# Fused attention and mixer kernel on one core: the transposes of the 64-key tile for two query tiles at a time, GpSimd's move taken out, and a new order

## The chip, the cores and the metric

The kernel runs on one core of one Trainium2 chip. The metric is the device time of one execution in microseconds (us); less is better. A core has five engines that run their own instruction streams and wait for each other through semaphores: TensorE (PE; its weight loads are listed apart as PEld), VectorE (DVE), ScalarE (ACT), GpSimd (POOL) and SyncE (SP, which here issues all DMAs).

## The reference, cut to what matters

```python
def _attn_ref(q, k, v, f):                  # B, H, S, D = 8, 8, 576, 64
    scores = np.matmul(q, k.transpose(0, 1, 3, 2)) / np.sqrt(D)
    cum = np.cumsum(np.log(np.clip(f, 0.0001, 1.0)), axis=-1)
    decay = cum[:, :, :, None] - cum[:, :, None, :]
    scores = np.where(causal, -1e9, scores + decay)     # causal: key after query
    attn = np.exp(scores - np.max(scores, axis=-1, keepdims=True))
    attn = attn / (np.sum(attn, axis=-1, keepdims=True) + 1e-09)
    return np.matmul(attn, v)

def _moe_ref(x, w_tok1, w_tok2, w_ch1, w_ch2):          # x: (8, 576, 512)
    h = np.maximum(x.transpose(0, 2, 1) @ w_tok1, 0.0) @ w_tok2     # 576 -> 256 -> 576
    u = x + h.transpose(0, 2, 1)
    return u + np.maximum(u @ w_ch1, 0.0) @ w_ch2                   # 512 -> 1536 -> 512
```

The 64 (batch, head) pairs go through causal attention with a decay; the result, laid out as (8, 576, 512), goes through a token-mixing and a channel-mixing block. The inputs are float32.

## The kernel before, in words

**Heads and tiles.** A loop in `build` goes over the 64 heads. The 576 positions of a head are five tiles: tile 0 has 64 positions, tiles 1 to 4 have 128 each. For each query tile `score` (L1061) makes the scores of all keys up to its end, `rmin` (L1068, DVE) adds the mask and takes the minimum, `expo` (L1075, ACT) writes the exponentials to a buffer `pr` and their sums, DVE makes reciprocals (L1093, L1096), and `norm` (L1103, POOL) multiplies the query tile's row of `pr` by its reciprocal: five instructions for a head, of 576, 448, 320, 192 and 64 columns.

**Transposes.** The product with `v` needs the normalised probabilities with keys on the partitions, so TensorE transposes them block by block (`tr`, L1117), a block being one query tile by one key tile: ten blocks for key tiles 1 to 4 (`trs`), and five for key tile 0. Of those five, the block of query tile 0 rides with the run of key tile 2, and `trs0` makes the other four, each 64 keys by 128 queries into one PSUM bank. There are 15 transposes for a head, 960 in all.

**Two parts of each number.** The matmuls take operands rounded to a shorter format, so 60 of the heads (all but the first four, called `fv` in the code) split a value into a high and a low part: ACT copies the transposed block from PSUM (high, `hi_act`, L729) and DVE subtracts that from PSUM (low, `lo_dve`, L738). Key tile 0 has only 64 keys, so its high part fills partitions 0 to 63 of a buffer `p0` and its low part is wanted in partitions 64 to 127, where one matmul (`av0`, L1189 and L1190) takes both. DVE writes the low part to a buffer `low` of 64 partitions, and POOL moves `low` to the upper half of `p0` (`hi_pool`, L732). `av0` waits for this move, and `avj` (L1197, L1199, L1201) adds the products of the other key tiles. In the first four heads nothing is split, and one copy suffices.

**The rest.** After every four heads of a batch `mixer` puts the token mixing and a part of the channel mixing of that batch into the same streams (L1683 to L1820). When the heads are done, the larger part of the channel mixing follows (L1544 to L1608). Weights are decoded and split by ACT, DVE and POOL beside the heads. `idle` (L803) puts small matmuls without use where the planner sees TensorE unoccupied.

**What sets the order.** `Plan.op` collects operations with a priority from the table `PR`; `Plan.run` simulates the engines and decides, for each engine, in which order the operations are written out; each buffer kind (`pr` has 3 buffers, `p0` and `low` have 1) is handed out on the way. In the kernel before, each engine takes, of the operations that are ready, the one with the lowest priority number.

## Time and profile before

| what | value |
|---|---|
| time, median of 3 runs | 1028.75 us (1024.6, 1028.75, 1030.69) |
| span of the profiled execution | 1021.2 us, 19368 instructions |
| PE busy | 1007.6 us, 99% |
| PEld busy | 882.6 us, 86% |
| DVE busy | 813.4 us, 80% |
| ACT busy | 694.8 us, 68% |
| POOL busy | 421.4 us, 41% |
| chain that ended last | PE 82%, DVE 7%, ACT 4%, POOL 2%, DMA 2%, issue 2% |

The own time of the profiled execution is not listed beside its span; the runs lie 3.4 to 9.5 us above the span, the median 7.5 us. The shares are means over two stages: in the first some 550 us the heads run, and all engines work; POOL has nothing after 600 us.

### The profile page before, as it was taken

The page shows a single profiled execution, that of the slowest core. Times are in us where ns is not written, and L with a number is a line of the kernel's source. Part 1 is how long each engine was busy: PE and PEld are TensorE (multiplying, and loading weights), DVE is VectorE, ACT ScalarE, POOL GpSimd, SP SyncE. Part 2 cuts the span into 40 slices and gives each one's busy share as a digit, 9 for nine tenths or more (in the row PEclk, how much of TensorE's full clock was granted, in tenths as well). Part 3 has the DMA queues.
Part 4 walks back from the last instruction along what each step waited for, and adds up shares of the span by engine and source line. Part 5 has one row for each costly group of instructions (what it writes and reads, how often), then busy time and mean ns, then how long its engine had stood idle before and what let it go on. Part 6 is the DMA issues. An engine that isn't in the chain of part 4 may idle for free.

```text
span 1021.2 us, 19368 instructions
## 1 busy us (share of the span) xinstructions
PE 1007.6 (99%) x6228; PEld 882.6 (86%) x6228; DVE 813.4 (80%) x1932; ACT 694.8 (68%) x1708; POOL 421.4 (41%) x530
## 2 busy tenths in 40 slices
PE   8999999999999999999999999999999999999998
PEld 6588998999999999999999988888888888888886
DVE  7789889888999887987896557959669766976694
ACT  6898888888988787878896444664375546544552
POOL 6689778687787686877881100000000000000000
PEclk9999999999999999999999999999999999999999
DMA  8765788876787766554665467825832762474154
GB/s 235 253 214 200 280 307 269 292 266 253 252 280 288 254 224 235 196 192 149 218 222 200 163 225 252 288 73 195 259 103 84 231 210 83 139 250 138 31 171 139
DMA packets 110597, 212.23 MB, mean 208 GB/s; under 512 B 13296, under 2 KB 51184, under 8 KB 109472
## 3 DMA queue, kind: packets, MB, share of 16 engines
q1 hardware_dynamic: 110496, 210.99, 61.4%
q8 instruction: 50, 0.82, 0.3%
q14 instruction: 51, 0.42, 0.1%
HBM read 113.26 MB, written 44.04 MB: 154 GB/s over the span
## 4 chain that ended last, share of the span: by engine, by line
PE 82%; DVE 7%; ACT 4%; POOL 2%; DMA 2%; issue 2%; SPq 0%; DVEq 0%; POOLq 0%; ACTq 0%
PE bank L1117 8%; PE bank L1606 6%; PE bank L1607 6%; PE bank L1544 6%; PE bank L1608 6%; PE bank L1545 6%; PE bank L1546 6%; PE bank L1061 5%; PE pair L1199 2%; PE pair L1061 2%; PE pair L1201 2%; ACT pr L1075 2%; PE bank L1785 2%; PE bank L1787 2%; PE bank L1786 2%
## 5 line engine op out<-in xcount | busy, mean ns | idle before, releaser
L1103 POOL TENSOR_SCALAR pr<-pr,rec 128x192 f32<-128x192 f32 (+4 forms) x320 | 165.6, 532 | 65.4 <-DVE rec L1096 27.3
L729 ACT ACTIVATE p<-bank 128x384 fp32r<-128x384 f32 (+3 forms) x300 | 129.1, 474 | 21.6 <-PE bank L1117 18.7
L1117 PE MATMUL bank<-ident,pr 128*128 128x128 f32 (+1 forms) x960 | 139.4, 274 | 1.8 <-DVE ring L738 1.0
L1075 ACT ACTIVATE pr<-bank,nmin 128x320 f32<-128x320 f32 (+3 forms) x256 | 118.3, 470 | 14.3 <-DVE nmin L1068 13.4
L1117 PEld LDWEIGHTS bank<-ident,pr 128*128 128x128 f32 (+1 forms) x960 | 106.4, 131 | 18.4 <-ACT pr L1075 2.5
L1068 DVE CUSTOM_DVE_ANT_0 bank<-bank,mask 128x448 f32<-128x448 f32 (+3 forms) x256 | 106.3, 434 | 14.5 <-PE bank L1061 9.4
L738 DVE TENSOR_TENSOR p<-bank,p 128x384 fp32r<-128x384 f32 (+1 forms) x180 | 105.0, 590 | 10.5 <-ACT p L729 9.4
L1606 PE MATMUL bank<-ring,w2r 128*128 128x512 f32 x242 | 94.2, 389 | 0.4 <-issue 0.4
L1607 PE MATMUL bank<-ring,w2r 128*128 128x512 f32 x242 | 94.2, 389 | 0.0
L1608 PE MATMUL bank<-ring,w2r 128*128 128x512 f32 x234 | 91.2, 390 | 0.0
L1061 PE MATMUL bank<-k 128*128 128x320 f32 (+1 forms) x480 | 83.1, 302 | 0.4 <-ACT pr L1075 0.2
L1201 PE MATMUL pair<-p,vv 128*128 128x512 f32 x240 | 75.6, 322 | 0.0
L980 POOL TENSOR_TENSOR hl<-raw,hl 128x1152 fp32r<-128x1152 f32 x27 | 72.3, 2678 | 1.1
L729 ACT ACTIVATE ring<-h 128x512 fp32r<-128x512 f32 x73 | 44.5, 628 | 41.3 <-PE bank L1608 16.0
L1199 PE MATMUL pair<-p,vv 128*64 128x512 f32 x240 | 69.4, 330 | 0.0
L729 ACT ACTIVATE ring<-xt 128x512 fp32r<-128x512 f32 (+1 forms) x83 | 52.3, 648 | 23.8 <-DVE xt L1512 8.4
L1061 PEld LDWEIGHTS bank<-k 128*128 128x128 f32 (+1 forms) x480 | 62.9, 176 | 3.9 <-DVE low L738 1.0
L738 DVE TENSOR_TENSOR low<-bank,p 64x512 fp32r<-64x512 f32 (+1 forms) x120 | 52.7, 443 | 8.8 <-ACT p L729 7.0
L729 ACT ACTIVATE ring<-bank 128x288 fp32r<-128x288 f32 (+2 forms) x96 | 46.9, 498 | 17.6 <-PE bank L1787 6.9
L1075 ACT ACTIVATE pr<-pair,nmin 128x576 f32<-128x576 f32 x64 | 47.3, 739 | 15.0 <-DVE nmin L1068 12.7
L735 POOL TENSOR_TENSOR ring<-xt,ring 128x576 fp32r<-128x576 f32 x32 | 45.8, 1439 | 21.6 <-ACT ring L729 20.4
L1606 PEld LDWEIGHTS bank<-ring,w2r 128*128 128x128 f32 x242 | 45.4, 188 | 10.3 <-ACT w2r L729 0.8
(197 smaller groups left out, 3046.9 us busy)
## 6 DMA issues: line engine op xcount, KB each, us to landing
k<-hl SPq DMA_DIRECT2D x180, 288.0 KB
w2r<-sd SPq DMA_DIRECT2D x80, 256.0 KB
raw<-in_qk SPq DMA_DIRECT2D x60, 288.0 KB
w2r<-wd SPq DMA_DIRECT2D x60, 256.0 KB
vr<-in_v SPq DMA_DIRECT2D x32, 320.0 KB
ud<-xt SPq DMA_DIRECT2D x8, 1152.0 KB
pd<-part SPq DMA_DIRECT2D x32, 288.0 KB
dd<-in_w_ch SPq DMA_DIRECT2D x12, 512.0 KB
```

The source lines that it names most:

```text
L729: nc.scalar.activation(out, in_, func, scale=scale)
L738: nc.vector.tensor_tensor(out, in_, asf(hi), op=ALU.subtract)
L1061: nc.tensor.matmul(ps[:m, of : of + w], k[:, 0, i0 : i0 + m], k[:, 1, j0 : j0 + w], start=(x == 0), stop=(fq or x == 1))
L1068: nc.vector.tensor_tensor_reduce(x, x, E["mask"][:m, a : a + w], -1.0 / D**0.5, 3e38, op0=ALU.add, op1=ALU.min, accum_out=E["nmin"][sm][:m ...
L1075: nc.scalar.activation(at(pr)[:m, poff[t] : poff[t] + w], at(buf)[:m, of : of + w], AF.Exp, bias=E["nmin"][sm][:m, t : t + 1], scale=-1.0, ...
L1103: nc.gpsimd.tensor_scalar(x, x, r, 0.0, op0=ALU.mult, op1=ALU.add)
L1117: nc.tensor.transpose(out, at(pr)[:, poff[i] + start[j] : poff[i] + end[j]], E["ident"])
L1199: nc.tensor.matmul(x[:D], at(vv)[:, v0 + j, :D], at(pb)[:, 1, c0 : c0 + w], start=False, stop=last)
L1201: nc.tensor.matmul(x, at(vv)[:, v0 + j, :], at(pb)[:, 0, c0 : c0 + w], start=False, stop=last)
L1606: nc.tensor.matmul(o_, wh[:, ms], h_, start=first and pr == 0, stop=False, skip_group_check=not first)
L1607: nc.tensor.matmul(o_, wl[:, ms], h_, start=False, stop=False, skip_group_check=not first)
L1608: nc.tensor.matmul(o_, wh[:, ms], l_, start=False, stop=pr == PH - 1, skip_group_check=not first)
```

## The change

The five transposes of key tile 0 become three. The blocks of query tiles 1 and 3 are put side by side, and so are those of 2 and 4: `norm` writes the 64 columns of key tile 0 of query tile 1 not in place but into 64 new columns of `pr` just ahead of query tile 3's row (and those of tile 2 ahead of tile 4's row). One transpose of 128 columns then takes the block of query tile 1 to partitions 0 to 63 and that of query tile 3 to partitions 64 to 127. The block of query tile 0 is a transpose of 64 by 64 (before, 128 rows of which half were zero). Of the result the lower PSUM half holds 320 queries and the upper half 256. ACT and DVE write the parts from each half straight to where they belong: the high part to the half that it came from, the low part to the other one. `low` and POOL's move are gone. `av0` is unchanged but for what it waits for.

For this `norm` becomes seven instructions for a head: 576, 448, 256, 128, 64 columns, and two more of 64 columns.

Beside it `Plan.run` is rewritten: each engine now takes its operations strictly by priority number, so `PR`, whose numbers are new, is the order itself. The number of small matmuls at the start is worked out from the planned start and no longer 112.

```diff
-    k19=(11, 23, 47, 59, 67, 77, 89, 104, 114, 142, 156, 174, 195, 211, 229, 256, 271, 285, 302, 328, 343, 360, 373, 394, 410, 421, 438, 455, 465, 478, 491, 502,),
...
+    poff = [sum(end[:t]) + T0 * max(0, t - 2) for t in range(NS)]
+    MID = T0 + 2 * P
...
-        def norm(t, sm=sm, pr=pr):
+        def norm(t, a, z, to, sm=sm, pr=pr):
             m = size[t]
-            x = at(pr)[:m, poff[t] : poff[t] + end[t]]
...
+            x, y = (at(pr)[:m, c : c + z - a] for c in (poff[t] + a, to))
+            nc.gpsimd.tensor_scalar(y, x, E["rec"][sm][:m, t // 2, t % 2 : t % 2 + 1], 0.0, op0=ALU.mult, op1=ALU.add)
...
         for t in (4, 3, 2, 1, 0):
+            a = T0 if t in (1, 2) else 0
+            p.op("POOL", d_pts(end[t] - a, 1), n + o["nrm"], lambda t=t, a=a, f=norm: f(t, a, end[t], poff[t] + a), rd=[("rec", sm)], wr=[(pr, t)], bufs=[pr])
+            if a:
+                p.op("POOL", d_pts(a, 1), n + o["nrm"], lambda t=t, a=a, f=norm: f(t, 0, a, poff[t + 2] - a), rd=[("rec", sm), (pr, t, "e")], wr=[(pr, t, "z")], bufs=[pr])
...
-                if first:
-                    tr(at(ps)[:T0, w : w + P], 0, 0)
...
-        def trs0(ps=ps, tr=tr):
-            for i in range(1, NS):
-                tr(at(ps)[:T0, (i - 1) * P : i * P], i, 0)
+        def trs0(ps=ps, pr=pr):
+            x, y = at(ps), at(pr)
+            nc.tensor.transpose(x[:T0, :T0], y[:T0, :T0], E["ident"][:T0, :T0])
+            for z in (0, 1):
+                nc.tensor.transpose(x[:, T0 + z * P : T0 + (z + 1) * P], y[:, poff[z + 3] - T0 : poff[z + 3] + T0], E["ident"])
...
+            for z, hs, ls, cs, ds in ((0, slice(0, T0), slice(T0, P), slice(0, MID), slice(0, MID)), (1, slice(T0, P), slice(0, T0), slice(MID, S), slice(T0, MID))):
+                w = cs.stop - cs.start
+                p.op("ACT", d_act(w), e0, lambda ps=ps, pb=p0_, hs=hs, cs=cs, ds=ds: hi_act(at(pb)[hs, cs], at(ps)[hs, ds]), rd=[ps], wr=[(p0_, "h", z)], bufs=[ps, p0_])
                 p.op(
...
+                    "DVE", d_dve(w), e0, lambda ps=ps, pb=p0_, hs=hs, ls=ls, cs=cs, ds=ds: lo_dve(at(pb)[ls, cs], at(ps)[hs, ds], at(pb)[hs, cs]),
...
-            p.op(
-                "POOL", d_pts(S) + 110, n + LAG + o["t0"] + o["lo0"], lambda pb=p0_, lb=low: hi_pool(at(pb)[T0:, :], asf(at(lb))),
-                rd=[(low, 0), (low, 1)], wr=[(p0_, "l")], bufs=[p0_, low],
-            )
...
+        for o in sorted(self.ops, key=lambda o: (o.prio, o.idx)):
+            queue[o.eng].append(o)
...
-                for _ in range(PRM["FILL"] if at_ == 0 else int((gap - g0) / g1) if gap > g2 else 0):
+                for _ in range(33 + int(max(0.0, o.start - 7500) / 66) if at_ == 0 else int((gap - g0) / g1) if gap > g2 else 0):
```

In the instruction lists, the useless matmuls (L803 before, L772 after) go from 166 to 95, GpSimd's instructions from 535 to 603, and the three memsets of `pr` at the start are gone; the counts of DVE, ACT and DMA instructions otherwise stay (the two copies and the two subtractions for key tile 0 are of 320 and 256 columns where they were of 512 and 64).

TensorE, before, in the middle of the heads: the end of one head (`pr_183`). The run of four 64-key transposes stands among the products with `v` (`pair_71` is their PSUM buffer, `p_186` to `p_190` the split parts, `k_176` and `k_178` the operands of the next scores). The `av0` that uses these four comes some rows later.

```order
L1117 MATMUL bank_65<-ident,pr_183 64x128 [waits DVE_49]
L1117 MATMUL bank_65<-ident,pr_183 64x128 x3
L1201 MATMUL pair_71<-p_186,vv_181 128x128
L1199 MATMUL pair_71<-p_186,vv_181 64x128
L1199 MATMUL pair_71<-p_186,vv_181 64x256
L1201 MATMUL pair_71<-p_186,vv_181 128x256
```

After, at the same head: one transpose of 64 by 64 and two of 128 by 128. `av0` (now L1140 and L1141) waits only for DVE where it waited for DVE and POOL.

```order
L1140 MATMUL pair_71<-p_190,vv_181 128x512 [waits DVE_49]
L1141 MATMUL pair_71<-p_190,vv_181 128x64
L1115 MATMUL bank_63<-ident,pr_183 64x64 [waits DVE_49,Pool_49]
L1117 MATMUL bank_63<-ident,pr_183 128x128 [waits Pool_49]
L1117 MATMUL bank_63<-ident,pr_183 128x128
```

What moved: two transposes fewer in this run and one fewer in that of key tile 2, one of the three at half the columns, and a wait for POOL that goes from `av0` to the transposes.

GpSimd, before, near the same place: the norms of one head (`pr_182`, L1103), the moves of two earlier ones (L732) and a split of `v` (L980).

```order
L1103 TENSOR_SCALAR pr_182<-pr_182,rec_92 128x192 [waits DVE_49,PE_49,Activation_49]
L1103 TENSOR_SCALAR pr_182<-pr_182,rec_92 128x576 [waits PE_49]
L1103 TENSOR_SCALAR pr_182<-pr_182,rec_92 128x448
L732 TENSOR_SCALAR p_190<-low_191 64x576 [waits DVE_49,Pool_49]
L980 TENSOR_TENSOR vv_181<-vr_174,vv_181 128x10x64 [waits PE_49,Activation_49,Pool_49]
L1103 TENSOR_SCALAR pr_182<-pr_182,rec_92 128x320
L1103 TENSOR_SCALAR pr_182<-pr_182,rec_92 64x64
L732 TENSOR_SCALAR p_190<-low_191 64x576 [waits DVE_49,Pool_49]
```

After: seven norms for a head (L1070; all seven of `pr_183` are in these rows), the heads' norms interleaved with each other and with the splits of `q` and `k` (L941, L949), and no moves.

```order
L1070 TENSOR_SCALAR pr_183<-pr_183,rec_91 128x576 [waits DVE_49]
L941 TENSOR_SCALAR hl_175<-raw_172 128x2x576 [waits DMAHW4_49,DMAHW5_49,DMAHW3_49,DMAHW6_49,DMAHW2_49,DMAHW7_49,DMAHW1_49,Pool_49]
L1070 TENSOR_SCALAR pr_183<-pr_183,rec_91 64x64
L1070 TENSOR_SCALAR pr_182<-pr_182,rec_92 128x448 [waits DVE_49,PE_49,Activation_49]
L949 TENSOR_TENSOR hl_175<-raw_172,hl_175 128x2x576 [waits Pool_49]
L1070 TENSOR_SCALAR pr_183<-pr_183,rec_91 128x448
L1070 TENSOR_SCALAR pr_183<-pr_183,rec_91 128x64
L1070 TENSOR_SCALAR pr_183<-pr_183,rec_91 128x256
L1070 TENSOR_SCALAR pr_182<-pr_182,rec_92 64x64
L1070 TENSOR_SCALAR pr_183<-pr_183,rec_91 128x64
L1070 TENSOR_SCALAR pr_182<-pr_182,rec_92 128x64 [waits Activation_49]
L1070 TENSOR_SCALAR pr_183<-pr_183,rec_91 128x128
```

What moved: the norms of query tiles 1 and 2 are two instructions each, and the move of 576 columns is no longer there.

SyncE, before, at the start of the program: the loads ahead of the first operands of the scores (`xt_151<-in_qk`); `in_w_tok` are weights, `raw_172` raw operands of later heads.

```order
L817 DMA dd<-in_w_tok 64x512
L994 DMA raw_172<-in_qk 64x1152
L817 DMA dd<-in_w_tok 64x512
L817 DMA dd<-in_w_tok 128x512 x3
L994 DMA raw_172<-in_qk 64x1152 [waits DMAHW0_49]
L1038 DMA xt_151<-in_qk 64x1152 [waits DMAHW1_49]
L1038 DMA xt_151<-in_qk 64x1152 [waits DMAHW2_49]
```

After, the same place:

```order
L786 DMA dd<-in_w_tok 64x512
L786 DMA dd<-in_w_tok 128x512
L786 DMA dd<-in_w_tok 64x512
L963 DMA raw_172<-in_qk 64x1152 x2
L1007 DMA xt_151<-in_qk 64x1152
L786 DMA dd<-in_w_tok 128x512 [waits DMAHW0_49]
L1007 DMA xt_151<-in_qk 64x1152 [waits DMAHW1_49]
```

What moved: two loads of weights (128 x 512 words, 256 KB each) that were ahead of the first `xt_151<-in_qk` come behind it. The third head's one-row loads `xt_151<-cc` (L1023) are the 19th and 20th rows of this queue before, and the 14th and 15th after.

## Rows read from the trace of the kernel before

**Rows 1.** The page's head and its busy line: engine, busy us, share, instructions.
```profile
span 1021.2 us, 19368 instructions
PE 1007.6 (99%) x6228; PEld 882.6 (86%) x6228; DVE 813.4 (80%) x1932; ACT 694.8 (68%) x1708; POOL 421.4 (41%) x530
```

**Rows 2.** Windows: stretch, its us, busy us by engine, clock granted, DMA share, GB/s.
```profile
0.00:26.00 26.00, 23.16 (x190) 17.86 (x190) 19.64 (x62) 17.73 (x48) 16.90 (x34) 1.00 0.80 236
...
200.00:300.00 100.00, 99.24 (x758) 92.99 (x758) 90.34 (x261) 87.59 (x246) 80.42 (x98) 1.00 0.78 271
300.00:400.00 100.00, 99.38 (x762) 94.19 (x761) 86.54 (x250) 81.47 (x227) 77.54 (x94) 1.00 0.70 246
...
800.00:900.00 100.00, 99.67 (x440) 82.15 (x439) 74.54 (x111) 50.79 (x88) 0.00 (x0) 1.00 0.53 168
...
1000.00:1021.00 21.00, 16.54 (x73) 13.35 (x72) 8.11 (x13) 3.16 (x5) 0.00 (x0) 0.96 0.37 128
```

**Rows 3.** Timeline of PE: start us, us to the last end, instruction, count.
```profile
259.99 0.29 PE L1815 MATMUL bank<-ring,held 128*128 128x288 f32 x1
260.27 0.50 PE L1189 MATMUL pair<-p,vv 128*128 128x512 f32 x1
...
263.12 1.80 PE L1117 MATMUL bank<-ident,pr 128*128 128x128 f32 x15
264.67 0.31 PE L1201 MATMUL pair<-p,vv 128*128 128x128 f32 x1
264.82 0.34 PE L1199 MATMUL pair<-p,vv 128*64 128x128 f32 x2
```

**Rows 4.** Groups by form: transposes of the probabilities, 128 and 64 keys wide.
```profile
L1117 PE MATMUL bank<-ident,pr 128*128 128x128 f32 x640 | 100.9, 275 | 1.0 <-DVE low L738 0.6 <-DVE ring L738 0.3
...
L1117 PE MATMUL bank<-ident,pr 128*64 128x128 f32 x320 | 55.1, 273 | 0.8 <-DVE ring L738 0.8
```

**Rows 5.** Timeline of PE: a matmul of 64 columns and its follower.
```profile
253.44 0.19 PE L1190 MATMUL pair<-p,vv 128*128 128x64 f32 x1
253.47 0.42 PE L1199 MATMUL pair<-p,vv 128*64 128x512 f32 x1
```

**Rows 6.** Timeline of PE and chain at the start: start us, us, what.
```profile
7.40 5.20 PE L803 MATMUL pair<-lower 128*16 128x128 f32 x79
13.00 1.25 PE L1061 MATMUL bank<-xt 97*64 97x64 f32 x4 [0.40 <-ACT dd L829]
...
19.53 2.02 PE L803 MATMUL pair<-lower 128*16 128x128 f32 x28
22.34 0.94 PE L1061 MATMUL bank<-xt 97*128 97x320 f32 x3 [0.79 <-DMA xt<-cc]
...
17.84 4.37 DMA xt<-cc
```

**Rows 7.** Groups by form, POOL's norms: count, busy us, mean ns, idle before and why.
```profile
L1103 POOL TENSOR_SCALAR pr<-pr,rec 128x576 f32<-128x576 f32 x64 | 47.9, 749 | 10.0 <-ACT p L729 6.0 <-DVE rec L1096 3.1 <-ACT ring L729 0.6
...
L1103 POOL TENSOR_SCALAR pr<-pr,rec 128x320 f32<-128x320 f32 x64 | 34.0, 532 | 8.3 <-ACT p L729 3.5 <-DVE rec L1096 2.4 <-PE bank L1117 1.6
L1103 POOL TENSOR_SCALAR pr<-pr,rec 128x192 f32<-128x192 f32 x64 | 27.1, 424 | 17.1 <-PE bank L1117 7.0 <-DVE rec L1096 5.0 <-ACT p L729 2.4
L1103 POOL TENSOR_SCALAR pr<-pr,rec 64x64 f32<-64x64 f32 x64 | 20.4, 319 | 12.1 <-ACT p L729 5.6 <-DVE rec L1096 2.5 <-ACT xt L1239 1.6
```

**Rows 8.** Tile `low`: POOL's move (ns min/median/max, first and last us), who waited.
```profile
L732 POOL TENSOR_SCALAR p<-low x60: 666/667/681, 59.0 to 546.4; 64x576 fp32r<-64x576 f32 x60
...
  PEld pair L1189: 2.1, 7
```

**Rows 9.** Groups by form, DVE's low parts of 64 partitions.
```profile
L738 DVE TENSOR_TENSOR low<-bank,p 64x512 fp32r<-64x512 f32 x60 | 40.7, 678 | 7.1 <-ACT p L729 6.1 <-POOL hl L980 0.2 <-POOL hl L972 0.2
L738 DVE TENSOR_TENSOR low<-bank,p 64x64 fp32r<-64x64 f32 x60 | 12.5, 209 | 1.7 <-ACT p L729 0.9 <-PE bank L1117 0.2
L738 DVE TENSOR_TENSOR ring<-bank,ring 64x256 fp32r<-64x256 f32 x16 | 6.7, 418 | 1.0 <-ACT ring L729 0.5
```

More of the change, by code (lines that the diff above doesn't have):

```diff
@@ L23 @@
 PR = dict(
-    k0=(0,),
+    k0=(1,),
     k1=(0, 1,),
@@ L555, in run @@
     def run(self, slots):
-        free = {k: None for k in slots}
-        busy_unit = {}
-        engines = {}
-        for o in self.ops:
-            engines.setdefault(o.eng, [])
-        ready = engines
-        engine_at = dict.fromkeys(engines, 0.0)
-        events = []
-        n = 0
-        for o in self.ops:
-            if not o.need:
-                ready[o.eng].append(o)
-                heapq.heappush(events, (o.ready, 0, 0))
-        heap_id = 1
-        t = 0.0
-        left = len(self.ops)
-        order = []
-        tail = port_at = 0.0
-        dma_at = 1000.0
-        ends, lands = [0.0] * 3, [0.0] * 8
-        nexts = {}
-        fifo = {}
+        queue = {e: [] for e in ("PE", "DVE", "ACT", "POOL", "SP")}
+        for o in sorted(self.ops, key=lambda o: (o.prio, o.idx)):
+            queue[o.eng].append(o)
+        head = dict.fromkeys(queue, 0)
+        engine_at = dict.fromkeys(queue, 0.0)
+        unit, nexts, fifo = {}, {}, {}
         for o in self.ops:
@@ new lines, in run @@
+        for _ in range(len(self.ops)):
+            best = None
+            for e, q in queue.items():
+                if head[e] == len(q) or q[head[e]].need:
+                    continue
+                x = place(q[head[e]])
+                if x is None:
+                    continue
+                t = max(x[0], port_at) if q[head[e]].port else x[0]
+                if best is None or t < best[0]:
+                    best = (t, e, x[1])
+            if best is None:
+                raise RuntimeError(f"no operation can start: {len(order)} of {len(self.ops)} placed")
+            t, e, got = best
+            o = queue[e][head[e]]
+            head[e] += 1
+            for b, s in got:
+                b.slot = s
+                k = self.GROUP.get(b.kind, b.kind)
+                if k in fifo:
+                    nexts[k] = fifo[k][b] + 1
+                for u in s:
+                    unit[u] = (0.0, None)
+            o.start = t
+            if e == "PE":
+                o.start = t + max(0.0, max(o.ready, t - tail) + o.head - t)
+                tail = o.tail
+            if e == "SP":
+                o.start = max(t, lands[-8] + 60)
+                end = max(o.start + o.dur, ends[-3])
+                dma_at = max(end + 270, dma_at) + o.lat
+                done = dma_at + 1400
+                lands.append(done)
+                if o.lat > 300:
+                    ends.append(dma_at)
+            else:
+                end = o.start + o.dur
+                done = end + o.lat
+            engine_at[e] = end
+            if o.port:
+                port_at = end
+            order.append(o)
+            for d in o.outs:
+                d.need -= 1
+                d.ready = max(d.ready, done + self.LAT[e][d.eng])
+            for b in o.bufs:
+                b.rel.append((done, e))
+                b.left -= 1
+                if b.left == 0:
+                    for u in b.slot:
+                        unit[u] = max(b.rel)
@@ L696, in build @@
     end = [a + b for a, b in zip(start, size)]
-    poff = [sum(end[:t]) for t in range(NS)]
+    poff = [sum(end[:t]) + T0 * max(0, t - 2) for t in range(NS)]
+    MID = T0 + 2 * P
     F2 = NF - F1
@@ L1866, in slots_of @@
         k["gt" + q] = [dd_units(5 * i, 4)]
[L1867 removed]
+    for kind in ("raw", "vr", "hl", "k1", "k2", "vv", "pr", "p34", "p2", "p1", "p0", "ring", "part", "xt"):
         k[kind] = [((kind, i),) for i in range(PRM[f"n_{kind}"])]
```

410 lines of the change are left out of this document (160 added, 250 removed).

## The prediction

> **What bounds the kernel now.** I read the page's busy line first: TensorE is busy in 1007.6 of 1021.2 us, so all recorded waiting of PE is 13.6 us [rows 1]. The windows say where the other engines stand beside it. While the heads run (200 to 400 us), PE is at 99%, but DVE is at 90 and 87%, ACT at 88 and 81%, POOL at 80 and 78%; after the heads (800 to 900 us) DVE is at 75%, ACT at 51%, and POOL has nothing [rows 2]. GpSimd's last move is at 546 us [rows 8], so the heads fill about the first 546 us, and only that stretch is touched. 4.5 us of PE's idle time are in the last 21 us, 2.8 us in the first 26 [rows 2]; neither is made of transposes.
>
> PE's 99% needs a second look, since the records overlap. The timeline shows it by start times. A matmul of 64 columns holds PE 0.03 us (253.44 to 253.47) [rows 5], so one of 288 columns should hold it 0.13; at 259.99 the next one starts only 0.28 us later, and it is an `av0`, which waits for POOL's move, with no idle time recorded [rows 3]. So PE does wait, in pieces of about 0.15 us that the busy line hides.
>
> The Trainium skill (Trainium Kernel Development and Optimization, Performance Expectations) says the same of matmul busy time, that it is a bad measure because matmuls are pipelined, and would have the share of weight loading read in its place. By that rule the heads, with PEld at 93 to 94 of 100 us, would be nearer to PE's limit than the late stage with 82 [rows 2]; the windows' busy shares of DVE and ACT say the reverse, and I do not go by it. What the hidden waiting would do to the gain is the first rival below.
>
> **The change part by part.** *Transposes.* At 263.12 the fifteen transposes of a head run back to back, those of 64 keys among them, and the second matmul after them starts at 264.82 [rows 3]. Of these 1.70 us, 0.06 belong to the one matmul of 128 columns between (twice 0.03); 1.64 / 15 = 0.109 us for each. Width does not matter: the two forms have means of 275 and 273 ns [rows 4]. A head loses five of these (0.545 us), and gets two of 128 by 128 (0.218) and one of 64 by 64. The trace has no f32 transpose of 64 columns. From above it costs as much as one of 128 columns, 0.109; from below as much as 64 columns of split operands, 0.03. I take half of 0.109, 0.055, since half the columns pass. A head saves 0.545 - 0.218 - 0.055 = 0.272 us, 64 heads 17.4 us; by the bounds 14.0 to 19.0 us.
>
> The Trainium skill (TensorE: Matmul & The Clock Gate, "Wait — 56ns, not 53.3ns?") gives the distance of matmuls as columns by 2.4 GHz and 2.5 ns more; if an f32 transpose is two such passes, as 0.109 us for 128 columns suggests, 64 columns are 58 ns, and the saving would be 17.2 us.
>
> This is work taken from the engine that is busy 99%, in the stretch in which the others are at 78 to 90%, so I count it in full, and what the others give back as a term of its own.
>
> *The move and the norms on POOL.* Sixty moves of 667 ns go [rows 8]. The norms of query tiles 1 and 2 shrink: 532 ns for 320 columns and 424 for 192 make 0.84 ns a column, so 256 and 128 columns are 478 and 370 ns; two instructions of 64 columns at 319 ns are new [rows 7]. A head's norms cost -54 - 54 + 638 = +530 ns; with the move gone a split head is 137 ns shorter: 60 x -0.137 + 4 x 0.53 = -6 us of POOL's 421.4. POOL is not on PE's path by its own load; what counts are the waits. PE's weight loads for `av0` waited seven times, 2.1 us together, for the move [rows 8]. They end; but the wait for POOL does not vanish, it goes to the run of three transposes, which needs all seven norms. I take half: -1 us, bounds 0 and -2.1.
>
> *Parts of key tile 0.* The same columns, cut 320 and 256 and no longer 512 and 64. On DVE 678 and 209 ns [rows 9] make 1.05 ns a column, so in place 477 and 410. The nearest row with the low part written to the other half of the partitions, 64 x 256 in the mixer's tile 0, takes 418 [rows 9]: 8 ns more. So 903 against 887 ns for a head, +1 us of DVE in all, covered by PE; uncovered, that 1 us. ACT's copies keep their columns and count; I take 0.
>
> *The start.* Two loads of 256 KB go behind the first operands of the scores. At the 236 GB/s of the first 26 us [rows 2] 512 KB are 2.2 us. In the trace PE fills the time to 13.00 and from 19.53 to 22.34 with matmuls without use, and the second stretch ends with the landing of `xt<-cc` [rows 6], whose issue is five places earlier in the new queue. So the start can shrink by 0 (another load takes its place) to 5 us (2.2 and the 2.8 from 19.53 to 22.34). I take -2. The 71 matmuls without use that go stood in such waits; 0 for them. The three memsets of `pr` go as well: 0.
>
> *What comes back as waiting.* If 17.4 us leave the 546 us, the other engines' shares rise by 3%: DVE from 90.3 to 93.3 in its fullest window. What this costs can be read from two windows: with DVE at 86.5 PE idles 0.62 us in 100, with DVE at 90.3 0.76 [rows 2]. Another three points would be 0.1 to 0.2 us in 100, some 0.8 us over the heads by the records; with the hidden pieces I take +2. Bounds: 0, and the whole saving.
>
> *The order.* All numbers are new, and the rule behind them too; the rows of the two orders show the same kinds of work at nearly the same places. Nothing says which way this goes, so 0, and 4 us either way for the range.
>
> Sum: -17.4 - 1 - 2 + 2 = -18.4 us. Against the profiled span that is 1021.2 to 1002.8 us; the median stands 7.5 us above the span, so the time is 1028.75 - 18.4 = **1010.3 us**, 1.8% less. The likeliest case has its own range of 1005 to 1016.
>
> **The rivals.** A measurement of this kernel can tell about 0.5% (5.1 us) from no change; its three runs lie 6 us apart.
>
> *First, the saving goes to waits.* If what paces the heads is the chain through DVE and ACT and not PE's own work, shorter transposes only make PE arrive earlier. For it: the hidden pieces of waiting, and DVE at 90%. Against: the idle time hardly differs between the windows with DVE at 90 and at 87%, and in neither is DVE full. Half of it gone is 1028.75 - 9 = 1020 us, all of it 1026 to 1029, no change.
>
> *Second, slower: the longer chain of norms.* Before its last transposes a head now needs seven norms and not five, 0.53 us more on POOL between the sums and the transposes. If PE waited for that in each split head, it would be 60 x 0.53 = 32 us, and the time 1028.75 - 18.4 + 32 = 1042 us. It is slower by over 0.5% from (18.4 + 5.1) / 60 = 0.39 us a head on. For it: POOL stands idle 8 to 17 us in front of each of these groups of norms, mostly for ACT and DVE [rows 7], so the norms start late in places. Against: POOL as a whole gets less to do, and is at 80% in its fullest window shown.
>
> *Third, the new order also takes out waiting.* PE idles or hides pieces all through the heads; an order that lets fewer of them happen saves more than the transposes. With 8 us more it is 1002 us. For it: the pieces are there [rows 3]; against: nothing in the rows of the order shows that they are fewer.
>
> *Fourth, the change does not do what it says*: the 64 by 64 transpose costs a full 0.109. Then 14.0 us, 1013.7, inside the likeliest case's range.
>
> **How the numbers follow.** The forecast with the fourth 0.62 (1005 to 1016), the third 0.15 (below 1005), the first 0.18 (0.10 for a part, 1016 to 1023.6, and 0.08 for no change), the second 0.05. Faster by over 0.5% is then 0.62 + 0.15 + 0.10 = 0.87, within 0.5% 0.08, slower 0.05. For eight times in ten I leave out the lower end of the third case and the upper of the first and all of the second: 1001 to 1021 us.
>
> **What would show each step.** In the new profile there are 832 transposes of the probabilities, 64 of them of 64 columns; PE's busy time is down by about 17 us, and the heads end about 18 us earlier (the last parts of key tile 0 at about 528 us, where the last move was at 546); the late stage takes as long as before. No POOL instruction writes `p`; POOL is busy about 415 us. A low part of 64 x 256 takes about 418 ns, one of 64 x 320 about 485. The first scores start about 2 us earlier. The forecast is wrong if PE's idle time, 13.6 us now, grows by 8 us or more, or if the waits for `pr` from POOL in front of the transposes come to tens of us; and too cautious if PE's busy time falls by clearly more than 17 us, since hidden waits are counted as busy.

## The result

The changed kernel took 1037.8 us (median of 4 runs, 1035.6 to 1039.7), the kernel before 1026.7 beside it: a ratio of 1.0106 with a 95% interval of 1.0073 to 1.0138. It is slower by 11 us, where 18 us less was forecast. Its profiled execution took 1035.64 us; the page's head and busy line:

```profile
span 1033.9 us, 18898 instructions
...
PE 1010.5 (98%) x6029; PEld 870.5 (84%) x6029; DVE 832.1 (80%) x1929; ACT 699.1 (68%) x1708; POOL 423.0 (41%) x598
```

TensorE has 199 instructions fewer than in [rows 1] and is busy 3 us longer, where 17 us less was forecast. It idles 1033.9 - 1010.5 = 23.4 us, 9.8 more than before; the prediction had named 8 us more as a sign that it is wrong. VectorE has three instructions fewer and is busy 18.7 us longer, so some of its instructions took more time.

The windows of the changed kernel, with the columns of [rows 2]:

```profile
0.00:26.00 26.00, 23.49 (x142) 15.97 (x142) 22.39 (x67) 18.82 (x51) 17.37 (x35) 1.00 0.78 222
...
100.00:200.00 100.00, 95.47 (x685) 87.64 (x684) 91.36 (x253) 84.45 (x226) 72.94 (x98) 0.97 0.77 266
200.00:300.00 100.00, 95.09 (x683) 86.73 (x682) 92.27 (x246) 85.94 (x234) 79.15 (x105) 0.97 0.78 272
300.00:400.00 100.00, 98.07 (x729) 90.42 (x728) 85.65 (x244) 82.19 (x220) 72.40 (x99) 1.00 0.61 209
...
800.00:900.00 100.00, 99.50 (x439) 81.96 (x438) 73.80 (x112) 48.40 (x87) 0.00 (x0) 1.00 0.54 169
...
293.60:300.40 6.80, 6.30 (x24) 5.83 (x25) 4.47 (x14) 4.74 (x14) 4.97 (x7) 0.50 0.39 149
```

The late stage is as in [rows 2]. The loss lies in the heads, whose last product with `v` ends at 566.0 us, where it ended at 552.2: between 200 and 300 us TensorE idles 4.9 us and not 0.8, and the mean granted clock there is 0.97 and not 1.00. The last row shows where that comes from: a stretch of 6.8 us at a granted clock of 0.5, the 1.2 GHz level.

The timeline of TensorE in the changed kernel, at the first scores, at one head's transposes of key tile 0, and around that slow stretch:

```profile
10.47 2.14 PE L1030 MATMUL bank<-xt 97*64 97x64 f32 x8
...
269.77 0.28 PE L1152 MATMUL pair<-p,vv 128*128 128x256 f32 x1
269.98 0.24 PE L1115 MATMUL bank<-ident,pr 64*64 64x64 f32 x1
270.15 0.44 PE L1117 MATMUL bank<-ident,pr 128*128 128x128 f32 x2
270.35 0.78 PE L1030 MATMUL pair<-k 128*128 128x288 f32 x4
...
290.05 0.28 PE L1668 MATMUL bank<-ring,held 128*128 128x256 f32 x1
294.10 0.77 PE L1140 MATMUL pair<-p,vv 128*128 128x512 f32 x1 [3.78 <-DVE p L707]
...
295.84 0.44 PE L1764 MATMUL bank<-ring,held 128*128 128x288 f32 x1
296.08 0.44 PE L1765 MATMUL bank<-ring,held 128*128 128x288 f32 x1
...
300.52 0.29 PE L1692 MATMUL bank<-held,ring 128*128 128x288 f32 x1
300.66 0.29 PE L1693 MATMUL bank<-held,ring 128*128 128x288 f32 x1
```

Three things are to be seen. The first scores start at 10.47 us, where they started at 13.00 [rows 6]. From the matmul in front of the 64 by 64 transpose to the instruction behind the two others (269.77 to 270.35) there are 0.58 us; by the prediction's prices it would be 0.12 + 0.055 + 0.218 = 0.39 at most. And behind the matmul of 290.05 TensorE is idle for 3.78 us, waiting for a low part from VectorE; in this wait, at 293.6, the granted clock falls to 0.5, and matmuls of 288 columns stand 0.24 us apart (295.84 to 296.08), where at full clock it is 0.14 (300.52 to 300.66).

What VectorE did meanwhile:

```profile
287.23 0.69 DVE L707 TENSOR_TENSOR p<-bank,p 128x512 fp32r<-128x512 f32 x1
287.84 4.29 DVE L802 TENSOR_SCALAR dd<-dd 128x512 uint32<-128x512 uint32 x1
292.16 0.43 DVE L707 TENSOR_TENSOR p<-bank,p 64x256 fp32r<-64x256 f32 x1
...
293.47 1.07 DVE L707 TENSOR_TENSOR p<-bank,p 64x320 fp32r<-64x320 f32 x2
```

And GpSimd in the same time:

```profile
287.74 1.15 POOL L941 TENSOR_SCALAR hl<-raw 128x1152 fp32r<-128x1152 f32 x1
288.87 0.37 POOL L1070 TENSOR_SCALAR pr<-pr,rec 128x128 f32<-128x128 f32 x1
289.21 2.63 POOL L949 TENSOR_TENSOR hl<-raw,hl 128x1152 fp32r<-128x1152 f32 x1
295.25 1.07 POOL L1070 TENSOR_SCALAR pr<-pr,rec 128x256 f32<-128x256 f32 x3 [3.41 <-DVE rec L1065]
```

L802 shifts a decoded piece of a weight, which usually takes 0.42 us. It started 0.10 us after GpSimd's L941 and ended at 292.13, 0.29 us after the third of three GpSimd instructions in a row. It has nothing to do with the transposes; but the two low parts of key tile 0 stand behind it in VectorE's queue, and TensorE waited for the second, of 64 x 320.

The tile `dd`'s decode instructions on VectorE in the kernel before (count, ns min/median/max, first and last start):

```profile
L833 DVE TENSOR_SCALAR dd<-dd x35: 270/409/958, 8.8 to 330.2; 128x512 uint32<-128x512 uint32 x22, 128x256 uint32<-128x256 uint32 x9, 128x288 uint32<-128x288 uint32 x4
L837 DVE SCALAR_TENSOR_TENSOR dd<-dd x35: 385/674/1891, 9.5 to 331.7; 128x512 uint32<-128x512 uint32 x22, 128x256 uint32<-128x256 uint32 x9, 128x288 uint32<-128x288 uint32 x4
```

and the same two in the changed kernel:

```profile
L802 DVE TENSOR_SCALAR dd<-dd x35: 269/416/4291, 6.8 to 297.4; 128x512 uint32<-128x512 uint32 x22, 128x256 uint32<-128x256 uint32 x9, 128x288 uint32<-128x288 uint32 x4
L806 DVE SCALAR_TENSOR_TENSOR dd<-dd x35: 411/680/3435, 8.2 to 307.8; 128x512 uint32<-128x512 uint32 x22, 128x256 uint32<-128x256 uint32 x9, 128x288 uint32<-128x288 uint32 x4
```

The medians are equal, the longest are not. The 70 instructions together took 37.3 us before and 50.2 after, none over 2 us before and three after. I call such a lengthening a stand-still, and count as its size what an instruction takes over the usual time of its form. The ends fit GpSimd as the cause: in the changed kernel and in after_full_rows (below) eleven of these instructions took over 1.4 us; all of them ran beside GpSimd, and each ended 0.28 to 0.32 us (L802, and the narrower ones of L806) or 0.55 us (L806 of 512 columns) after the end of a GpSimd instruction, as if its own work had begun only then. The Trainium skill (SBUF — State Buffer, SBUF: two separate sides) has a reason for it: VectorE's second pair of ports is GpSimd's only one, and whoever starts first among certain VectorE instructions and GpSimd's holds it for its whole instruction. The trace agrees with the blocking, but VectorE stood still through three GpSimd instructions and not one. This page was not weighed in the prediction.

### The profile page after: what moved, and what is told of

It reads as the page before. It is cut to its first block, busy times and chain, and to the rows that moved or that the text cites. A ratio compares the mean times of both kernels' runs of the same rounds, so it can differ in the third digit from the quotient of the medians.

```text
span 1033.9 us, 18898 instructions
## 1 busy us (share of the span) xinstructions
PE 1010.5 (98%) x6029; PEld 870.5 (84%) x6029; DVE 832.1 (80%) x1929; ACT 699.1 (68%) x1708; POOL 423.0 (41%) x598
## 4 chain that ended last, share of the span: by engine, by line
PE 75%; DVE 12%; ACT 8%; issue 3%; DMA 2%; SPq 0%; ACTq 0%; DVEq 0%
PE bank L1495 6%; PE bank L1496 6%; PE bank L1497 6%; PE bank L1557 5%; PE bank L1558 5%; PE bank L1559 5%; PE bank L1030 5%; PE bank L1084 5%; DVE p L707 4%; ACT p L698 3%; ACT pr L1044 2%; PE pair L1150 2%; PE pair L1152 2%; PE pair L1030 2%; PE bank L1117 2%
## 5 line engine op out<-in xcount | busy, mean ns | idle before, releaser
L1070 POOL TENSOR_SCALAR pr<-pr,rec 128x64 f32<-128x64 f32 (+5 forms) x448 | 209.0, 485 | 71.6 <-DVE rec L1065 48.2
L707 DVE TENSOR_TENSOR p<-bank,p 128x384 fp32r<-128x384 f32 (+3 forms) x300 | 160.1, 539 | 29.5 <-ACT p L698 24.7
L698 ACT ACTIVATE p<-bank 128x384 fp32r<-128x384 f32 (+3 forms) x300 | 139.6, 477 | 28.3 <-PE bank L1117 11.7
L1037 DVE CUSTOM_DVE_ANT_0 bank<-bank,mask 128x320 f32<-128x320 f32 (+3 forms) x256 | 107.7, 430 | 8.4 <-PE bank L1030 6.3
L1084 PE MATMUL bank<-ident,pr 128*128 128x128 f32 x640 | 100.7, 276 | 3.9 <-DVE ring L707 1.9
L1559 PE MATMUL bank<-ring,w2r 128*128 128x512 f32 x248 | 96.5, 389 | 0.0
L1084 PEld LDWEIGHTS bank<-ident,pr 128*128 128x128 f32 x640 | 75.9, 141 | 16.4 <-issue 5.9
L1557 PE MATMUL bank<-ring,w2r 128*128 128x512 f32 x224 | 87.2, 389 | 0.5 <-ACT ring L698 0.5
L1558 PE MATMUL bank<-ring,w2r 128*128 128x512 f32 x224 | 87.1, 389 | 0.0
L949 POOL TENSOR_TENSOR hl<-raw,hl 128x1152 fp32r<-128x1152 f32 x27 | 72.6, 2689 | 0.4
L949 POOL TENSOR_TENSOR vv<-vr,vv 128x640 fp32r<-128x640 f32 x30 | 47.9, 1595 | 29.2 <-ACT vv L939 29.2
L1495 PE MATMUL bank<-ring,w1r 128*128 128x512 f32 x150 | 58.5, 390 | 0.0
L1496 PE MATMUL bank<-ring,w1r 128*128 128x512 f32 x150 | 58.4, 389 | 0.0
L698 ACT ACTIVATE ring<-bank 128x512 fp32r<-128x512 f32 (+2 forms) x96 | 46.4, 497 | 12.9 <-PE bank L1668 5.1
```

What stands on the lines that cost most here:

```text
L698: nc.scalar.activation(out, in_, func, scale=scale)
L707: nc.vector.tensor_tensor(out, in_, asf(hi), op=ALU.subtract)
L949: (nc.gpsimd if eng == "POOL" else nc.vector).tensor_tensor(out, in_, asf(hi), op=ALU.subtract)
L1070: nc.gpsimd.tensor_scalar(y, x, E["rec"][sm][:m, t // 2, t % 2 : t % 2 + 1], 0.0, op0=ALU.mult, op1=ALU.add)
L1084: nc.tensor.transpose(out, at(pr)[:, poff[i] + start[j] : poff[i] + end[j]], E["ident"])
L1495: nc.tensor.matmul(q, wh[:, cs], h_, start=first and c == 0, stop=False, skip_group_check=not first)
```

## The experiments

Four suspects came out of the two traces: the 64 by 64 transpose, the stand-stills, VectorE and ScalarE as what paces the heads, and the new order as a whole. All ratios below are to the kernel before, run beside.

**The new operations under the old order** (change_old_order). The planner's old rule and the old priority numbers, the two new norms and the new parts next to their old neighbours (here a few lines of the edit, against the changed kernel):

```diff
-    k29=(15, 18, 24, 25, 31, 33, ...
+    k29=(19, 21, 26, 23, 30, 32, ...
...
-        queue = {e: [] for e in ("PE", "DVE", "ACT", "POOL", "SP")}
...
+        free = {k: None for k in slots}
...
```

> The three transposes, seven norms and direct parts of the change, but the planner's rule and the priorities of the kernel before (a new operation takes the number of the one it comes from). Theory A (the change itself saves TensorE's 17 us, and the new order loses about 30 in waits): 1007 to 1016 us. Theory B (the heads are paced by VectorE and ScalarE, so a shorter TensorE gains nothing in any order): 1023 to 1031 us. Theory C (the longer chain of norms on GpSimd costs the time): 1035 us or more.

It took 1049.0 us, ratio 1.025 (1.0223 to 1.0278): the slowest of all, with no decode instruction over 1.42 us. Theory C named such a time, but its chain of norms is not what the waits show: TensorE's weight loads for transposes waited 3.5 us in all for GpSimd's `pr`. So the new order is not what spoiled a good change; the new operations are slower in the old order than in the new one.

**The decode's shift in another form**, in both kernels (after_plain_shift, before_plain_shift):

```diff
-            nc.vector.tensor_scalar(g, g, 3, None, op0=ALU.logical_shift_left)
+            nc.vector.tensor_scalar(low, low, 29, None, op0=ALU.logical_shift_right)
...
-            nc.vector.scalar_tensor_tensor(g, low, 29, g, op0=ALU.logical_shift_right, op1=ALU.bitwise_or)
+            nc.vector.scalar_tensor_tensor(g, g, 3, low, op0=ALU.logical_shift_left, op1=ALU.bitwise_or)
```

> The changed kernel, but the decode's first VectorE instruction shifts the low words in place (strided, one input) and not the result (contiguous), and the second one makes up for it; the same values come out. Theory A with the collision as the main loss (VectorE's decode instructions are held up while GpSimd works, up to 4.3 us each): no shift lasts over 1 us, VectorE's busy time falls by some 5 to 10 us, no stretch at half the clock, 1018 to 1028 us. Rival (the long shifts are a sign and not a cause): within 4 us of the changed kernel's 1037.8.

> The same edit of the decode on the kernel before, where no shift lasted over 0.96 us. Theory A: no collisions to lose, and 0.2 us more for each of 35 shifts: within 5 us of the kernel before, either way. If it gains as much as on the changed kernel, the collision doesn't tell the two orders apart.

1039.5 us, ratio 1.0154 (1.0124 to 1.0184), and 1024.0, ratio 1.0 (0.9987 to 1.0012). The edit did not do what it was for: the longest such instruction still took 4.35 us. So the times tell nothing about what the stand-stills cost, though that of the changed kernel is the rival's.

**The saving given back** (after_pe_given_back): the transposes of key tile 0 of the changed kernel done twice.

```diff
+            for z in (0, 1):
-            nc.tensor.transpose(x[:T0, :T0], y[:T0, :T0], E["ident"][:T0, :T0])
+                nc.tensor.transpose(x[:T0, :T0], y[:T0, :T0], E["ident"][:T0, :T0])
-            for z in (0, 1):
+            for z in (0, 1, 0, 1):
```

> The changed kernel with its three transposes of key tile 0 done twice: TensorE gets its 17.4 us of work back, nothing else changes. If TensorE's work still sets the time in the new order: 1050 to 1056 us. If the heads wait for other engines there: 1038 to 1043 us.

1044.3 us, ratio 1.0193 (1.0152 to 1.0235), some 6.5 us over the changed kernel (9 by the two ratios) for 17.4 us of TensorE's work, between the two theories. TensorE's work sets the time only in part.

**The 64 by 64 transpose, taken out and put in** (after_full_rows, before_64x64). In the changed kernel it goes back to 128 rows, the lower ones zero (the three memsets of `pr` come back for that, not shown); in the kernel before, the first transpose of key tile 0 becomes 64 by 64:

```diff
 after_full_rows
-            nc.tensor.transpose(x[:T0, :T0], y[:T0, :T0], E["ident"][:T0, :T0])
+            nc.tensor.transpose(x[:T0, :P], y[:, :T0], E["ident"])
 before_64x64
-                    tr(at(ps)[:T0, w : w + P], 0, 0)
+                    nc.tensor.transpose(at(ps)[:T0, w : w + T0], at(pr)[:T0, :T0], E["ident"][:T0, :T0])
```

> The 64 by 64 transpose of the changed kernel is done over all 128 rows again (the rows below 64 hold zeros), all else as in the changed kernel. Theory S (the transpose of 64 rows is dear on TensorE: it and its two neighbours take about 0.17, 0.17 and 0.09 more, where 0.055 and 0.109 were reckoned): about 0.21 us a head less, 13.6 us of TensorE's work; the transposes behind it take 0.109 again and the matmul before it is not longer. If TensorE's work sets the time wholly, 1024; as in the run where 17.4 us of it given back cost 6.5, 1032; so 1024 to 1033. Theory D (what costs are the waits for VectorE and ScalarE, whose work is the same): 1035 to 1039, with TensorE idle for as much longer as it works less.

> One part of the change alone, in the kernel before: its first transpose of key tile 0 takes 64 rows and 64 columns instead of 128 by 64. Theory S: about 0.21 us a head more (64 heads, 13.6 us), 1031 to 1038, with the two neighbours of that transpose longer. Theory that such a transpose costs about half of one of 128 columns, as in the prediction: 64 times 0.055 less, 3.5 us: 1019 to 1024.

1034.7 us, ratio 1.0069 (1.0038 to 1.0101), and 1033.7, ratio 1.0076 (1.0046 to 1.0106). TensorE's timeline in after_full_rows, at the same place of another head:

```profile
274.43 0.28 PE L1152 MATMUL pair<-p,vv 128*128 128x256 f32 x1
274.54 0.27 PE L1115 MATMUL bank<-ident,pr 128*64 128x128 f32 x1
274.65 0.38 PE L1117 MATMUL bank<-ident,pr 128*128 128x128 f32 x2
274.79 0.38 PE L1030 MATMUL pair<-k 128*128 128x288 f32 x1
```

The stretch that took 0.58 us takes 0.36 here (274.43 to 274.79), with twice the columns. The same in before_64x64:

```profile
260.36 0.55 PE L1117 MATMUL bank<-ident,pr 128*128 128x128 f32 x3
260.83 0.24 PE L1134 MATMUL bank<-ident,pr 64*64 64x64 f32 x1
261.00 0.40 PE L1785 MATMUL bank<-ring,held 128*128 128x288 f32 x1
261.24 0.29 PE L1786 MATMUL bank<-ring,held 128*128 128x288 f32 x1
261.38 0.30 PE L1787 MATMUL bank<-ring,held 128*128 128x288 f32 x1
```

Three transposes of 128 rows take 0.47 us up to the 64 by 64 one, not 3 x 0.109 = 0.33; this takes 0.17; and the matmul behind it 0.24 where the next takes 0.14. By the start times it is the same in all 64 heads of both kernels: the instruction of 64 rows takes 0.17 itself, the one in front of it 0.09 to 0.1 longer than usual, the one behind it 0.05 to 0.1. By the two stretches of 0.58 and 0.36 us it is 0.22 us a head more than the form with twice the rows and columns, 14 us of TensorE's work in 64 heads. In time that was 8.7 us in the kernel before, and about 3 in the changed one, where the two intervals overlap. The theory that it costs half is refuted: 1019 to 1024 was expected of it.

The kernel before had the price in its own trace, in the first four heads, where `av0` works on 64 rows:

```profile
28.10 0.27 PE L1190 MATMUL pair<-part,vr 64*64 64x64 f32 x2
28.30 1.28 PE L1061 MATMUL bank<-xt 97*64 97x64 f32 x4
```

The first of these two is followed by its like and takes 0.056 us by the start times, about half of 0.109; the second is followed by one of 97 rows and takes 0.149. With two transposes of 64 by 64 in a row (after_pe_given_back) they take 0.08 and 0.146. So what is dear, by these rows, is the change to another number of rows and back, and not the smaller transpose as such.

**The decode's two instructions made harmless** (after_full_no_decode, before_no_decode; after_full_memset). First cut to one column of 512, in after_full_rows and in the kernel before; then, in after_full_rows, replaced by instructions of full width that read nothing:

```diff
 no_decode
-            nc.vector.tensor_scalar(g, g, 3, ...)
+            nc.vector.tensor_scalar(g[:, :1], g[:, :1], 3, ...)
-            nc.vector.scalar_tensor_tensor(g, low, 29, g, ...)
+            nc.vector.scalar_tensor_tensor(g[:, :1], low[:, :1], 29, g[:, :1], ...)
 memset, in place of each of the two
+            nc.vector.memset(asf(g), 0.0)
```

> As after_full_rows, and VectorE's two instructions for each decoded piece of the weights work on one column instead of 512 (the weights' low bits are left undone; all counts of instructions stay). Theory C (VectorE's instruction stands still for up to 4 us while GpSimd works, TensorE waits for that, and its granted clock falls to half behind): 8 to 13 us below after_full_rows, the granted clock 1.0 up to the last stage. Theory that these are harmless: within 3 us of after_full_rows.

> The kernel before with the same cut of VectorE's two instructions to one column. Theory C: 0 to 4 us below the kernel before, since its longest such instruction took 0.96 us and its clock did not fall; what it gains here is what less work on VectorE is worth without collisions, and is to be taken off the gain of the changed kernel. If it gains as much as the changed kernel does (8 us or more), the gain comes from less work on VectorE and not from collisions.

> after_full_rows with VectorE's two instructions for each decoded piece replaced by two that set all its 512 columns to zero (they read nothing; the decoded weights are zero). VectorE's work stays near what it was. Theory C (instructions that read and write SBUF on VectorE are held up by GpSimd): 1016 to 1024 as in after_full_no_decode, and no such instruction over 1 us. Theory that after_full_no_decode gained by less work on VectorE: 1030 to 1036. If the zeroing instructions are held up too (one of them over 2 us), this run tells nothing between the two.

1019.1 us, ratio 0.9959 (0.9925 to 0.9993), and 1021.5, ratio 0.9963 (0.9944 to 0.9982): by the medians the cut is worth 15.6 us in after_full_rows and 3.4 in the kernel before, by the ratios 11 and 4 (8 to 13 and 0 to 4 were expected). So 8 to 12 us of it are not the work; from the widths of the intervals I estimate that this is known to some 5 us either way. Not every stand-still is gone:

```profile
L806 DVE SCALAR_TENSOR_TENSOR dd<-dd x35: 105/160/2897, 7.9 to 292.9; 128x1 uint32<-128x1 uint32 x35
```

The one of 2.90 us, on a single column, ends 0.02 us after a GpSimd instruction. And two of the eight executions had a mean granted clock of 0.991 and 0.993 and took 1028.8 and 1025.3 us. The weights come out wrong in these runs, so TensorE works on other numbers too; but they do so in before_no_decode as well, and that gained 3.4.

With memset 1017.4, ratio 0.993 (0.9915 to 0.9946), though VectorE has nearly as much to do (28.6 us in these instructions, where without stand-stills they would take about 35); there the two lines read

```profile
L802 DVE MEMSET dd<- x35: 272/485/485, 6.8 to 283.2; 128x512 f32 x22, 128x256 f32 x9, 128x288 f32 x4
L806 DVE MEMSET dd<- x35: 272/485/485, 8.3 to 291.5; 128x512 f32 x22, 128x256 f32 x9, 128x288 f32 x4
```

Not one is lengthened, and the granted clock is 1.00 in all windows of the heads, as here from 200 to 300 us:

```profile
200.00:300.00 100.00, 98.51 (x742) 91.34 (x741) 92.99 (x266) 90.02 (x242) 78.28 (x107) 1.00 0.74 263
```

GpSimd's busy time falls too, from 419.5 us in after_full_rows to 411.1 with memset, so GpSimd seems to lose too where the two meet.

**TensorE's work taken off, nothing else** (before_two_fewer): in the kernel before, two of the four transposes of 0.109 us at the end of a head are left out.

```diff
-            for i in range(1, NS):
+            for i in (2, 4):
                 tr(at(ps)[:T0, (i - 1) * P : i * P], i, 0)
```

> The kernel before, two of the four 0.109 us transposes at the end of each head left out (the parts behind them then hold what stood in the bank before): 14 us of TensorE's work less and nothing else changed. Theory P, the prediction's own step (work taken off TensorE shows in the time one to one): 1011. Theory W (VectorE and ScalarE are so near behind that TensorE then waits for them): less than two thirds of it, 1016 to 1024.

1022.4 us, ratio 0.9985 (0.9965 to 1.0005): 14 us of TensorE's work are worth 2.3 us, and no change is inside the interval, which reaches from 3.6 us less to 0.5 more. (The order of the other instructions was made for the longer run; another order was not tried.) Its windows:

```profile
200.00:300.00 100.00, 97.60 (x729) 89.68 (x727) 89.53 (x261) 86.69 (x244) 78.53 (x96) 1.00 0.77 270
300.00:400.00 100.00, 98.58 (x745) 92.19 (x744) 87.89 (x253) 81.81 (x227) 79.20 (x95) 1.00 0.69 246
```

VectorE and ScalarE do what they did [rows 2], at the same pace; TensorE does less and idles more. The busy line shows only a part of it. Estimated from the start times (each matmul's distance to the next, less the usual distance of its form), TensorE's waits of all kinds in the first 620 us are 42 us in the kernel before and 56 here: the 14 us, all but whole. Both figures hang on what is taken as usual; with median distances they differ by 13 us. The chain of before_two_fewer, by engine:

```profile
PE 75%; DVE 8%; ACT 8%; issue 3%; DMA 3%; POOL 2%; SPq 0%; ACTq 0%; DVEq 0%; POOLq 0%
```

TensorE's share is 75%, where the kernel before had 82% (the table of the profile before); what it lost went to ScalarE above all. In the changed kernel the same line is

```profile
PE 75%; DVE 12%; ACT 8%; issue 3%; DMA 2%; SPq 0%; ACTq 0%; DVEq 0%
```

and in after_full_memset, the fastest kernel of all,

```profile
PE 68%; DVE 14%; ACT 11%; issue 4%; DMA 3%; POOL 1%; SPq 0%; ACTq 0%; DVEq 0%
```

So the shares say that waits for other engines lie on the chain, and not what they cost. Nor does VectorE's work alone pace the heads: in before_no_decode VectorE is busy 793.4 us and not 813.4, and the time fell by 3.4.

**The old order once more, with full rows** (old_order_full_rows: change_old_order with the edit of after_full_rows).

> change_old_order (the new operations under the old order) with the transpose of 64 rows done over all 128 rows. Theory S: 8 to 14 us below change_old_order, 1035 to 1041, still slower than the kernel before, since the other waits of the old order stay. Theory that the order alone made change_old_order slow: 1046 to 1050.

1046.7 us, ratio 1.0235 (1.0205 to 1.0264). Theory S, 1035 to 1041, did not come: of change_old_order's 25 us over the kernel before only 2.3 go with the 64 by 64 transpose, and the two intervals overlap. It has few stand-stills (some 2 us in all), and its chain reads

```profile
PE 66%; ACT 14%; DVE 13%; issue 4%; POOL 2%; DMA 2%; SPq 0%; ACTq 0%; DVEq 0%; POOLq 0%
```

That is near the shares of after_full_memset, so it does not tell what makes the old order slow; which of the new operations stand badly in it was not tried.

**Six places moved, nothing left out** (full_rows_moved_8, after_moved_8, full_rows_moved_12). Of the decode instructions that stood still, six get numbers 4 to 8 places later in VectorE's order (up to 12 in the last run), and one that has to follow them goes along; the computation is whole:

```diff
 in full_rows_moved_8 and after_moved_8
-    k14=(..., 291, 290, ..., 465, ..., 531, 558, ...)
+    k14=(..., 299.1, 298.1, ..., 473.1, ..., 535.1, 566.1, ...)
```

(Two numbers of `k15` move as well, and full_rows_moved_12 has larger ones, not shown.)

> after_full_rows, with six of VectorE's 70 instructions of the decode set 4 to 8 places later in VectorE's own order (the ones that stood still for 1.4 to 4.6 us while GpSimd worked on a key block or a copy of the rows of x); nothing is left out. Theory C (it is these stand-stills that cost): if the places behind are free of GpSimd's long instructions, 1016 to 1024, as where the two instructions were replaced; the longest decode instruction under 2 us and the granted clock at 1.0 through the heads. If new stand-stills come at the new places, no gain (1030 to 1036). Theory that the gain of the runs without the decode came from VectorE's smaller work: 1030 to 1036 even where the stand-stills are gone.

> The changed kernel itself, its 64 by 64 transposes kept, with the same six places moved. Theory C: 10 to 14 us below the changed kernel, 1024 to 1028; against full_rows_moved_8 the transposes of 64 rows then cost what they cost with TensorE less held up, 3 to 9 us.

> As full_rows_moved_8, with 12 places for 8 (11 for the one by 7). Theory C: 1016 to 1026 if no new stand-still; decoded pieces come 2 us later, which GpSimd and ScalarE may wait for.

1031.3 us, ratio 1.0063 (1.0043 to 1.0082); 1038.0, ratio 1.0124 (1.0097 to 1.015); 1038.2, ratio 1.014 (1.011 to 1.0169). The two decode lines of full_rows_moved_8:

```profile
L802 DVE TENSOR_SCALAR dd<-dd x35: 269/417/2827, 6.7 to 292.2; 128x512 uint32<-128x512 uint32 x22, 128x256 uint32<-128x256 uint32 x9, 128x288 uint32<-128x288 uint32 x4
L806 DVE SCALAR_TENSOR_TENSOR dd<-dd x35: 411/678/1785, 8.2 to 301.5; 128x512 uint32<-128x512 uint32 x22, 128x256 uint32<-128x256 uint32 x9, 128x288 uint32<-128x288 uint32 x4
```

The stand-stills moved rather than went: one of 2.8 us stays, and in all there are some 10 us of them (20 in after_full_rows, 13 with 12 places). The expected 1016 to 1024 did not come, so this theory is not shown by a kernel that computes everything. The profiled execution, with no slow stretch in the heads, took 1027.5 us, but the kernel's twelve runs lie between 1025.8 and 1036.8. The two fastest had a mean granted clock of 1.000, the ten others of 0.995 to 0.998; so a place that is free in one execution seems not to be in the next, which the one profile does not show. What the pair does show is the 64 by 64 transpose: after_moved_8, expected at 1024 to 1028, is 6.8 us above full_rows_moved_8, with intervals that do not touch.

## Why the prediction was wrong, point by point

**The transposes, "so I count it in full".** This is the step that failed. It took TensorE's 99% as proof that work taken from it comes off the time. before_two_fewer took 14 us off and got 2.3. TensorE's own waits were already some 42 us by start times, not the 13.6 of the busy line, and they grew by what was saved: in the heads the engines wait for each other, with VectorE at 90% and ScalarE at 88% [rows 2]. Which of them sets the pace is not shown; 20 us less work on VectorE alone gave 3.4. The prediction had seen such hidden pieces [rows 3] and named this as its first rival, with 0.18; the argument against it (idle time hardly differs between VectorE at 86.5 and at 90.3) was read from the same busy line that it had just called blind.

**"What comes back as waiting", +2.** The term for this very effect was sized from those two windows. Measured in before_two_fewer, some 12 of 14 us come back, which its upper bound, the whole saving, allowed for.

**"One of 64 by 64 ... I take half of 0.109".** Half is what it takes among its like (0.056 us). Where it stands it is not, and it is outside the bounds of 0.03 and 0.109: with what it does to its neighbours it costs about 0.22 us more than the transpose of 128 rows, 14 us of work in 64 heads. Two transposes less save 0.218 us a head, so the change takes next to nothing off TensorE. In time the form was worth 3 to 9 us (after against after_full_rows, the two moved kernels, before_64x64), and 2.3 in the old order, where none is not excluded. The bounds came from instructions among their like; the trace of before has matmuls of 64 rows next to ones of other heights only in the first four heads, and they were not looked at. The Trainium skill (TensorEngine Tiling (Array Packing), Key Properties) says that a change of tiling mode drains TensorE. It names no price; the trace agrees, with the three lengthened instructions above, if a transpose of 64 rows counts as another mode.

**"The order ... so 0, and 4 us either way".** The order brought decode instructions of VectorE to where GpSimd works on long pieces. Making these instructions harmless was worth 11 to 17 us, of which some 4 are less work by the kernel before: 8 to 14 us, at least twice the bound. In the profiled execution two of the waits, 2.8 and 3.8 us, and two stretches of 6.8 us at half the clock that begin in them, make 6.6 + 2 x 3, nearly 13 us by estimate. (At 0.24 us a matmul for 0.14, a stretch of 6.8 us at the lower level holds the work of about 4.) Both engines' busy shares were in the windows; that their instructions could hold each other up was not asked.

**What was right.** The start: first scores 2.5 us earlier, for 2. VectorE's parts of key tile 0: 0.43 us for 64 x 256, forecast 0.42, and 484 ns for 64 x 320, forecast 485. The late stage did not change. The second rival, the longer chain of norms on GpSimd, did not happen: in the list of TensorE's waits none for GpSimd's `pr` comes to 0.3 us, and the weight loads of L1115 waited 1.1 us for it in all heads together. GpSimd's busy time was missed: forecast 415 us, measured 423.0, and 411.1 with memset.

**The sum.** Forecast -18.4, measured +11. Work of 14 us taken off TensorE alone is worth about 2, the 64 by 64 form costs 3 to 9, the stand-stills 8 to 14. The parts do not add exactly, since a wait that one makes hides what another costs. With both taken out, what stays of the idea is between nothing and some 4 us. With the same cut of the decode, after_full_no_decode and before_no_decode took 1019.1 and 1021.5 us, at ratios of 0.9959 and 0.9963; after_full_memset took 1017.4, and its interval still touches that of before_no_decode. The start, 2.5 us earlier, is in these figures too.

**What stays open.** Why the new operations lose 25 us in the old order; which engine sets the pace of the heads; what the stand-stills cost in a kernel that computes everything; and whether an order exists that keeps the stand-stills out in every execution. No version with the whole computation beat the kernel before.

## What to carry to other kernels

An engine at 99% is not by that alone the bound: take some of its work out and nothing else, and see whether the time follows, before counting on a saving. A smaller instruction among larger ones can be dearer than the larger one; price it with the instructions before and behind it, from starts and not from durations. When an order is made anew, look for the longest instance of each short instruction, not its median: a few stand-stills in front of a wait decide more than the mean.

## What the hardware showed

- A transpose of 64 rows and 64 columns between instructions of 128 rows takes 0.17 us itself, the instruction in front of it 0.09 to 0.1 and the one behind it 0.05 to 0.1 longer (after, before_64x64, 64 heads each); one of 128 rows and 128 columns in its place takes 0.11 and lengthens none (after_full_rows). A 64 by 64 matmul followed by its like took 0.056 (before).
- A VectorE instruction of 0.42 us that reads and writes SBUF took up to 4.6 us beside GpSimd (after_full_rows), through several GpSimd instructions in a row, and ended 0.28 us after the last of them; zeroing instructions of the same width stayed at 0.485 us, all 44 of them.
- In a wait of TensorE of 3.78 us the granted clock fell to 0.5 (the 1.2 GHz level) and stayed there for 6.8 us, although TensorE was busy in 6.3 of them (after).
